# A fused attention, channel-mix and two-factor kernel: four-byte gate reads taken out of the load queue, and three numbers of the planner changed

## The chip, the core and the metric

One core of a Trainium2 chip runs the whole program. The metric is device time in microseconds, the median of several runs; lower is better. The engines are TensorE (PE, with its weight loads PEld beside it), VectorE (DVE), ScalarE (ACT), GpSimd (POOL) and SyncE (SP). SP computes nothing here: it issues every DMA of the kernel, one after the other, and each may first wait on semaphores.

## What is computed

Three blocks follow each other, on 4 batches of 576 positions:

```python
# 1: windowed attention, 8 heads of 64; heads 0-3 plain window of 32, heads 4-7 dilated by 4
scores = np.where(masks, scale * np.matmul(q, k.transpose(0, 1, 3, 2)), -1000000000.0)
attn = softmax(scores)                       # written out with max, exp, sum
x = np.matmul(attn, v)                       # -> x: (4, 576, 512)
# 2: channel mix with a shift by one position
xk = mu_k * x + (1.0 - mu_k) * x_prev
xr = mu_r * x + (1.0 - mu_r) * x_prev
k = np.maximum(xk @ w_k, 0.0)
x = sigmoid(xr @ w_r) * (k * k @ w_v)
# 3: a rank-32 product along the sequence, then two dense layers
u = x + (x.transpose(0, 2, 1) @ U @ V).transpose(0, 2, 1)
return u + np.maximum(u @ w_ch1, 0.0) @ w_ch2
```

The weights arrive as 64-bit numbers. The kernel turns them into fp32 itself, and splits most operands into a high and a low fp32r part, so that one product is three matmuls.

## The kernel before

The work of block 2 is cut into 8 chunks of 288 positions (two for each batch), that of block 3 into 5 groups of positions. Attention is cut into 32 units (a batch, one of two parts of the sequence, a pair of heads); units 0 to 3 run one by one in `attend`, the others in pairs in `attend2`. Chunk 0 of block 2 is multiplied in fp32 as it is (`L829` for the four r rows, `L813` for the k and v tiles); from chunk 1 on the split operands are used (`L816` to `L818`). So the first chunk needs only the 20 converted weight pieces (called W0 to W19 below; 512 KB of 64-bit words each), and the later ones need high and low parts of them (`L351`, `L348`).

One conversion is one ACT instruction (`L384`) and four on DVE (`L385`, `L386`, `L388`, `L391`). A k tile of chunk 0 needs four pieces, W4 to W7 for the first half of the tiles and W8 to W11 for the second; the v tiles need W12 to W15 and then W16 to W19.

The inputs come through `load`: q and k of a unit (`L522`, tile `raw`), v of a unit (`L525`, same tile), a weight piece (`L367`, tile `w`), the constants and mu. `raw` and `w` have four buffers each. A new unit's load must wait until PE has used up an old unit (`L603` or `L716`, the product with v); a new weight piece must wait until DVE has finished an old conversion (`L391`). From the 5th load to the 28th, `load` issues a gate first (`L336`): a DMA of four bytes, read out of the tile that the load four places earlier fills, which SP can issue only when that load has landed. So SP never runs more than four loads ahead there. Besides the gates, SP waits before a DMA when the DMA eight places earlier has not landed (semaphores `DMAHW0` to `DMAHW7` in the orders below).

Every instruction is recorded as an `op` with an expected duration, and `plan` sets the order. It simulates the five engines, picks on each engine among the next 160 operations the one that can start first or that is most urgent, and repeats that ten times with due times from the pass before. The order that it finds is the order in which the program is written; at run time each engine works its own list in that order, and waits where an operand is missing. In the planner a DMA takes size / `RATE`, one after the other, and a tile's buffer counts as free 40 ns after the last use of the tile that held it.

Near the end of block 2 and in group 0 of block 3 the converted `w_ch1` and `w_ch2`, parked in DRAM as `w2f`, come back (`L444`, tile `st`) and are combined for a seven-product scheme by DVE (`L471`), ACT (`L351`, `ch`) and POOL (`L346`, `cl`); `ug` (`L970`) holds a group of u, from which the operands `tr`, `tA` and `tB` are made.

Of the kernel before, what the change touches and what calls it, by code (L numbers as in the profile page):

```python
# [9 lines left out]
I32 = mybir.dt.int32  # L10
# [6 lines left out]
P = 128  # L17
# [8 lines left out]
QW, KW = 64, 96  # L26
# [6 lines left out]
NALL = NMASK + len(TWO)  # L33
# [18 lines left out]
QKW, VW = 640, 640  # L52
# [13 lines left out]
SLACK = 100.0  # L66
SLACK_PE = 100.0

OUTSTANDING = 4
GATED = 28  # L70
PLAN_PRINT = None
PASSES = 10
RATE = 245.0


@with_exitstack
def tile_attention_mix_channel(
    ctx: ExitStack, tc: tile.TileContext, qk0, qk1a, qk1b, v0, v1, cst, mu, w1raw, w2raw, upk, vpk, out
):
    nc = tc.nc  # L80
# [7 lines left out]
    cst_t = cp.tile([P, P + NALL * KW], F32, name="cst_t")  # L88
    ident = cst_t[:, 0:P]
    masks = [cst_t[:, P + i * KW : P + (i + 1) * KW] for i in range(NALL)]  # L90
    mu_t = cp.tile([P, 8], F32, name="mu_t")
# [7 lines left out]
    ops = []  # L99
# [21 lines left out]
    def op(eng, ns, fn, r=(), w=(), more=100, lock=False, mode=None, size=0):  # L121

        o = Op()
        o.eng, o.ns, o.fn, o.r, o.w, o.more, o.lock, o.mode, o.size = eng, ns, fn, list(r), list(w), more, lock, mode, size
        ops.append(o)

    def plan():
# [28 lines left out]
        def x_end(x):  # L156
            if x.end is not None:
                return x.end
            end = 0.0
            for u in reversed(x.ops):  # L160
                if u.done is None:
                    return NEVER
                end = max(end, u.done)
            x.end = end
            return end

        def ready(o):
            t = 0.0
            for d in o.deps:
                if d.done is None:  # L170
                    return None
                t = max(t, d.done + 40)
            if getattr(o, "behind", None) and o.behind.done is None:
                return None
            for x in o.tiles:
                if x.ops[0] is not o and x.ops[0].done is None:
                    return None
            for x in o.first:
                if x.at and x.line[x.at - 1].ops[0].done is None and x.line[x.at - 1].ops[0] is not o:
                    return None  # L180
                ends = sorted((x_end(y) for y in x.line[: x.at]), reverse=True)
                if len(ends) >= x.bufs:
                    if ends[x.bufs - 1] == NEVER:
                        return None
                    t = max(t, ends[x.bufs - 1] + 40)
            return t

        def forward(rank):
# [12 lines left out]
            while len(order) < len(ops):  # L201
# [32 lines left out]
                if e == "SP":  # L234
                    begin = max(t + 1300, dma)
                    dma = begin + o.size / RATE
                    o.done = dma + 700
# [85 lines left out]
    def dma(nbytes, fn, r, w):  # L323
        op("SP", 415, fn, r, w, size=nbytes)

    landing = []
    gate_d = tc.dram_tile([1, 64], I32, name="gate_d")

    def load(nbytes, fn, key, at):

        k = len(landing)
        landing.append((key, at))
        gate = None
        if OUTSTANDING <= k < GATED:
            seen, where = landing[k - OUTSTANDING]
            op("SP", 415, lambda: nc.sync.dma_start(gate_d[:, k : k + 1], where().bitcast(I32)[0:1, 0:1]),  # L336
               [seen], [("gate", k)], size=4)
            gate = ops[-1]
        dma(nbytes, fn, [], [key])
        ops[-1].behind = gate  # L340

    def sub(eng, n, out_, a, b, r, w, psum=False, fr=True):

# [20 lines left out]

    def cv_load(src, n):
        raw = Lazy([P, CW], I64, "w64", "w64", 4)
        load(P * n * 8, lambda: nc.sync.dma_start(raw()[:, :n], src), (raw,), lambda: raw())  # L367
        return raw

    def cv_bits(raw, n, xt_=None):  # L370
# [135 lines left out]
    def unit(u):  # L506
        part_i, pair = divmod(u, NPAIR)
        b, part = divmod(part_i, 2)
        return b, part, pair

    def a_load(u, which=("qk", "v")):
        b, part, pair = unit(u)
        nw, kc = unit_kind(pair, part)[:2]
        if part == 0:
            src, vsrc = qk0[b * NPAIR + pair], v0[b * NPAIR + pair]
        else:
            src, vsrc = (qk1a if pair < 2 else qk1b)[b * 2 + pair % 2], v1[b * NPAIR + pair]
        if u not in raws:
            raws[u] = Lazy([P, QKW + VW], F32, "raw", "raw", 4)
        raw = raws[u]  # L520
        if "qk" in which:
            load(P * 4 * (nw * QW + kc), lambda: nc.sync.dma_start(raw()[:, : nw * QW + kc], src),  # L522
                 (raw, "qk"), lambda: raw())
        if "v" in which:
            load(KW * 4 * 2 * nw * D, lambda: nc.sync.dma_start(raw()[:KW, QKW : QKW + 2 * nw * D], vsrc),  # L525
                 (raw, "v"), lambda: raw()[:, QKW:])

    def attend(u):
        b, part, pair = unit(u)
# [641 lines left out]
    def next_piece():  # L1171
        src, k, _ = jobs[len(loaded)]
        loaded.append(cv_load(src, k))

    a_load(0, ["qk"])
    load(P * 4 * (P + NALL * KW), lambda: nc.sync.dma_start(cst_t, cst), ("cst",), lambda: cst_t)
    next_piece()
    a_load(0, ["v"])
    load(P * 32, lambda: nc.sync.dma_start(mu_t, mu), ("mu",), lambda: mu_t)
    a_load(1, ["qk"])  # L1180
    next_piece()
    a_load(1, ["v"])
# [213 lines left out]
```

## Time and profile before

| | |
|---|---|
| device time, median of 3 runs | 775.2 us (773.4 to 776.62) |
| profiled execution: device time | 775.23 us |
| profiled execution: span | 773.3 us, so 1.93 us lie around it |
| PE busy | 740.0 us (96%) |
| PEld busy | 678.2 us (88%) |
| DVE busy | 580.5 us (75%) |
| ACT busy | 404.8 us (52%) |
| POOL busy | 396.1 us (51%) |
| mean granted clock of TensorE | 0.991 |

The shares are averages over stages with different limits: up to about 90 us attention, conversions and chunk 0 overlap; then the chunks 1 to 7 follow, and from about 360 us on block 3. A row of a timeline gives start and length of an instruction or of several equal ones, with the idle time ahead of it on its engine and what ended it in brackets.

### The profile page before, as it was taken

The numbers are of one execution on the slowest core, as the hardware profiler recorded it, in microseconds if no ns is written. First come the engines' busy times: TensorE is split into PE (matmuls) and PEld (weight loads), VectorE is DVE, ScalarE is ACT, GpSimd is POOL, SyncE is SP. The second block draws the span as 40 slices with busy tenths as digits, with TensorE's granted clock in tenths as the row PEclk, the third lists the DMA queues.
The fourth block names the chain that finished last, engine by engine and source line by source line (L and its number), as shares of the span: only waits on it lengthen the run. The fifth ranks groups of instructions, "written<-read, shape, count | busy, mean of one in ns | idle before, by whom it ended". The sixth has DMA issues, their size and how long they took to land. (4 is left out here: it accounts for less than half of the span.)

```text
span 773.3 us, 16141 instructions
## 1 busy us (share of the span) xinstructions
PE 740.0 (96%) x5784; PEld 678.2 (88%) x5784; DVE 580.5 (75%) x1302; ACT 404.8 (52%) x1019; POOL 396.1 (51%) x404
## 2 busy tenths in 40 slices
PE   4798999999999999999999999999999999999998
PEld 3566899999999999999898899889988999898986
DVE  5889989999999963556467889876797974665632
ACT  4578778767767765454345444443544343333310
POOL 1333236455646564355367668544677754455600
PEclk9989999999999999999999999999999999999999
DMA  8677627759685720345652344123442312032001
GB/s 251 207 230 227 202 71 236 231 169 288 207 271 177 235 90 31 106 129 178 202 196 79 103 155 141 54 89 97 144 135 69 122 56 82 29 110 82 28 1 54
DMA packets 54255, 107.56 MB, mean 139 GB/s; under 512 B 5920, under 2 KB 16032, under 8 KB 54176
## 3 DMA queue, kind: packets, MB, share of 16 engines
q1 hardware_dynamic: 54176, 106.54, 42.8%
q8 instruction: 45, 0.74, 0.4%
q14 instruction: 34, 0.28, 0.1%
HBM read 83.97 MB, written 22.54 MB: 138 GB/s over the span
## 5 line engine op out<-in xcount | busy, mean ns | idle before, releaser
L346 POOL TENSOR_TENSOR cl<-sums,ch 128x512 fp32r<-128x512 f32 x72 | 99.6, 1383 | 82.5 <-ACT ch L351 57.2
L1116 PE MATMUL psS<-hl,rh 128*128 128x512 f32 (+1 forms) x320 | 119.5, 373 | 2.0 <-DVE hl L1052 2.0
L1114 PE MATMUL psS<-hh,rh 128*128 128x512 f32 (+1 forms) x320 | 119.5, 374 | 1.7 <-ACT hh L1051 0.9
L1115 PE MATMUL psS<-hh,rl 128*128 128x512 f32 (+1 forms) x320 | 119.0, 372 | 0.0
L351 ACT ACTIVATE ch<-sums 128x512 fp32r<-128x512 f32 (+1 forms) x104 | 57.1, 561 | 113.3 <-DVE sums L471 104.7
L816 PE MATMUL psM<-xk,wh 128*128 128x288 f32 x336 | 101.2, 301 | 0.4 <-DVE y L878 0.4
L817 PE MATMUL psM<-xk,wl 128*128 128x288 f32 x336 | 99.1, 295 | 0.0
L818 PE MATMUL psM<-xk,wh 128*128 128x288 f32 x336 | 98.8, 294 | 0.0
L471 DVE TENSOR_TENSOR sums<-st 128x256 f32<-128x256 f32 (+1 forms) x144 | 90.5, 675 | 8.7 <-POOL cl L346 5.9
L346 POOL TENSOR_TENSOR cl<-st,ch 128x256 fp32r<-128x256 f32 x80 | 68.8, 876 | 54.6 <-PE psM L1039 31.4
L346 POOL TENSOR_TENSOR xk<-m,xk 128x288 fp32r<-128x288 f32 x56 | 52.4, 949 | 50.6 <-ACT xk L351 39.9
L1116 PEld LDWEIGHTS psS<-hl,rh 128*128 128x128 f32 x320 | 60.3, 188 | 14.0 <-DVE hl L1052 2.4
L1114 PEld LDWEIGHTS psS<-hh,rh 128*128 128x128 f32 x320 | 60.3, 188 | 12.2 <-DVE us L950 1.1
L346 POOL TENSOR_TENSOR k2s<-k,k2s 128x288 fp32r<-128x288 f32 x49 | 44.0, 900 | 48.8 <-ACT k2s L351 47.5
L1115 PEld LDWEIGHTS psS<-hh,rl 128*128 128x128 f32 x320 | 60.3, 189 | 9.5
L816 PE MATMUL psM<-k2s,wh 128*128 128x288 f32 x224 | 67.5, 301 | 0.0
L817 PE MATMUL psM<-k2s,wl 128*128 128x288 f32 x224 | 66.0, 295 | 0.0
L818 PE MATMUL psM<-k2s,wh 128*128 128x288 f32 x224 | 65.9, 294 | 0.0
L816 PEld LDWEIGHTS psM<-xk,wh 128*128 128x128 f32 x336 | 63.0, 188 | 1.4 <-DVE y L878 0.9
L818 PEld LDWEIGHTS psM<-xk,wh 128*128 128x128 f32 x336 | 63.2, 188 | 0.0
L817 PEld LDWEIGHTS psM<-xk,wl 128*128 128x128 f32 x336 | 63.1, 188 | 0.1
L1074 DVE TENSOR_TENSOR ok<-ok,psM 128x256 f32<-128x256 f32 (+1 forms) x96 | 46.4, 503 | 20.3 <-PE psM L1039 18.5
(156 smaller groups left out, 2146.8 us busy)
## 6 DMA issues: line engine op xcount, KB each, us to landing
st<-w2f SPq DMA_DIRECT2D x96, 256.0 KB, 3.1
w<-w2raw SPq DMA_DIRECT2D x32, 512.0 KB, 5.2
w<-w1raw SPq DMA_DIRECT2D x20, 512.0 KB, 5.2
w2f<-w SPq DMA_DIRECT2D x32, 256.0 KB
raw<-qk SPq DMA_DIRECT2D x16, 320.0 KB, 4.5
ytmp<-y SPq DMA_DIRECT2D x32, 144.0 KB, 2.1
yb<-ytmp SPq DMA_DIRECT2D x4, 1152.0 KB, 6.4
uf<-us SPq DMA_DIRECT2D x32, 144.0 KB, 2.4
```

The source lines that it names most:

```text
L346: op("POOL", t, lambda: nc.gpsimd.tensor_tensor(out=out_(), in0=a(), in1=b(), op=ALU.subtract), r, w, 40, lock=True)
L351: act(n, lambda: nc.scalar.activation(out_(), in_(), AF.Copy), r, w, psum, strided)
L471: dve(k * Q, lambda: nc.vector.tensor_tensor(out=q(sm_, n, k)(), in0=a(), in1=b(), op=op_), [(s1,), (s2,)], [(sm_, key)], two=True)
L816: nc.tensor.matmul(a, lhsT=wh, rhs=xh, start=start, stop=False)
L817: nc.tensor.matmul(a, lhsT=wl, rhs=xh, start=False, stop=False)
L818: nc.tensor.matmul(a, lhsT=wh, rhs=xl, start=False, stop=stop)
L1074: dve(k * Q, lambda: nc.vector.tensor_tensor(out=out_(), in0=a(), in1=b(), op=op_), r, w, two=True, psum=True)
L1114: nc.tensor.matmul(a, lhsT=wh, rhs=xh, start=(j == 0 and e == 0), stop=False)
L1115: nc.tensor.matmul(a, lhsT=wl, rhs=xh, start=False, stop=False)
L1116: nc.tensor.matmul(a, lhsT=wh, rhs=xl, start=False, stop=(j == 7 and e == 1))
```

## The change

The gates go, with the list of loads that they needed and the planner's rule that a load stands behind its gate. `RATE` goes from 245 to 285 GB/s. In `ready`, a tile first written by SP (a load of any kind into a reused buffer) is now taken to have its buffer 1,500 ns after the last use of the old tile instead of 40 ns; other engines keep 40. At run time nothing waits for these 1,500 ns: they only shape the order. Buffers, operations and sizes stay as they are, and every other line below `load` moves up by 15.

```diff
-OUTSTANDING = 4
-GATED = 28
+LATE = 1500.0
...
-RATE = 245.0
+RATE = 285.0
...
-            if getattr(o, "behind", None) and o.behind.done is None:
-                return None
...
-                    t = max(t, ends[x.bufs - 1] + 40)
+                    t = max(t, ends[x.bufs - 1] + (LATE if o.eng == "SP" else 40))
...
-    landing = []
-    gate_d = tc.dram_tile([1, 64], I32, name="gate_d")
-
-    def load(nbytes, fn, key, at):
-
-        k = len(landing)
-        landing.append((key, at))
-        gate = None
-        if OUTSTANDING <= k < GATED:
-            seen, where = landing[k - OUTSTANDING]
-            op("SP", 415, lambda: nc.sync.dma_start(gate_d[:, k : k + 1], where().bitcast(I32)[0:1, 0:1]),
-               [seen], [("gate", k)], size=4)
-            gate = ops[-1]
+    def load(nbytes, fn, key):
+
         dma(nbytes, fn, [], [key])
-        ops[-1].behind = gate
```

Since the order is planned anew, it moves on all engines. Three places follow; in the rows of the change a line number is 15 lower than that of the same line before.

On SP, from the load of W5 on (before). `w_333` is W5, `w_449` is W6; the two `qk1b` loads are units 6 and 7.

```order
L367 DMA w_333<-w1raw 128x512 [waits DVE_49,Activation_49]
L336 DMA gate_d<-w_285 1x1 [waits DMAHW5_49,DMAHW4_49]
L336 DMA gate_d<-raw 1x1 [waits DMAHW7_49]
L522 DMA raw<-qk1b 128x640 [waits DMAHW6_49,PE_49]
L525 DMA raw<-v 96x512
L336 DMA gate_d<-raw 1x1 [waits DMAHW1_49,DMAHW0_49]
L336 DMA gate_d<-w_333 1x1 [waits DMAHW3_49]
L522 DMA raw<-qk1b 128x640 [waits DMAHW2_49,PE_49]
L525 DMA raw<-v 96x512
L336 DMA gate_d<-raw 1x1 [waits DMAHW6_49,DMAHW4_49]
L367 DMA w_449<-w1raw 128x512 [waits DMAHW5_49,DVE_49,Activation_49]
```

The same stretch of the change: `w_307` is W5, `w_347` to `w_440` are W6 to W9, `qk1a` is unit 5.

```order
L352 DMA w_307<-w1raw 128x512 [waits DMAHW1_49,DVE_49,Activation_49]
L507 DMA raw<-qk1a 128x544 [waits DMAHW2_49,PE_49]
L510 DMA raw<-v 96x512 [waits DMAHW3_49]
L507 DMA raw<-qk1b 128x640 [waits DMAHW4_49,PE_49]
L510 DMA raw<-v 96x512 [waits DMAHW5_49]
L352 DMA w_347<-w1raw 128x512 [waits DMAHW6_49,DVE_49,Activation_49]
L352 DMA w_353<-w1raw 128x512 [waits DMAHW7_49,DVE_49,Activation_49]
L352 DMA w_425<-w1raw 128x512 [waits DMAHW0_49,DMAHW1_49,DVE_49,Activation_49]
L352 DMA w_440<-w1raw 128x512 [waits DVE_49]
L507 DMA raw<-qk1b 128x640 [waits DMAHW2_49,PE_49]
```

W5 now stands ahead of unit 5, and W6 to W9 stand ahead of unit 7 instead of behind it.

On PE, from the scores of units 6 and 7 to the first product of chunk 1 (before). `L654` are scores, `L699` transposes, `L716` products with v, `L813` with `xk` the k tiles and with `k` the v tiles.

```order
L654 MATMUL psS<-raw 64x96 x16
L813 MATMUL psM<-xk_248,wx 128x288 x16
L699 MATMUL psS<-cst_t,pr 96x128 x8
L716 MATMUL psS<-pts,raw 64x64 x16
L654 MATMUL psS<-raw 64x96 x20
L813 MATMUL psM<-xk_248,wx 128x288 x16
L813 MATMUL psM<-k_615,wx 128x288 x16
L699 MATMUL psS<-cst_t,pr 96x128 x10
L716 MATMUL psS<-pts,raw 64x64 x20
L654 MATMUL psS<-raw 64x96 x20
L813 MATMUL psM<-k_615,wx 128x288 x16
L816 MATMUL psM<-xk,wh 128x288
```

The same in the change:

```order
L639 MATMUL psS<-raw 64x96 x16
L798 MATMUL psM<-xk_239,wx 128x288 x16
L684 MATMUL psS<-cst_t,pr 96x128 x8
L798 MATMUL psM<-xk_239,wx 128x288 x4
L701 MATMUL psS<-pts,raw 64x64 x16
L639 MATMUL psS<-raw 64x96 x20
L798 MATMUL psM<-xk_239,wx 128x288 x12
L798 MATMUL psM<-k_610,wx 128x288 x8
L684 MATMUL psS<-cst_t,pr 96x128 x10
L798 MATMUL psM<-k_610,wx 128x288 x8
L701 MATMUL psS<-pts,raw 64x64 x20
L639 MATMUL psS<-raw 64x96 x20
```

Four matmuls of the k tiles now stand between transposes and the product with v, and eight of the v tiles behind the next transposes; the scores of units 6 and 7 keep their place among the tiles.

On SP in group 0 of block 3, from the `st` load of piece 10 of `w_ch1` (`w2f_80`) to `yb` of batch 2 (before):

```order
L444 DMA st<-w2f_80 128x512
L953 DMA uf<-us 128x288
L444 DMA st<-w2f_76 128x512
L444 DMA st<-w2f_81 128x512
L953 DMA uf<-us 128x288
L970 DMA ug<-uf 128x4x512
L953 DMA uf<-us 128x288
L444 DMA st<-w2f_79 128x512
L444 DMA st<-w2f_80 128x512
L953 DMA uf<-us 128x288 x2
L900 DMA yb<-ytmp_68 128x4x576
L444 DMA st<-w2f_82 128x512
```

The same in the change:

```order
L429 DMA st<-w2f_80 128x512
L429 DMA st<-w2f_81 128x512
L938 DMA uf<-us 128x288
L955 DMA ug<-uf 128x4x512
L429 DMA st<-w2f_76 128x512
L938 DMA uf<-us 128x288 x3
L429 DMA st<-w2f_79 128x512
L885 DMA yb<-ytmp_68 128x4x576
L429 DMA st<-w2f_80 128x512
L1113 DMA ot<-uf 128x256 x2
L429 DMA st<-w2f_82 128x512
```

`ug` has moved ahead of one `st` load; the second `st` load of piece 10 has moved behind `yb`, and two `ot` loads ahead of piece 12.

## Rows read from the trace of the kernel before

**Rows 1.** The page's DMA issues: operands, count, KB each, median us to landing.

```profile
st<-w2f SPq DMA_DIRECT2D x96, 256.0 KB, 3.1
...
yb<-ytmp SPq DMA_DIRECT2D x4, 1152.0 KB, 6.4
```

**Rows 2.** Busy time by stage: stretch, length, PE PEld DVE ACT POOL, clock, DMA share, GB/s.

```profile
0.00:43.44 43.44, 28.02 (x284) 20.93 (x284) 29.57 (x105) 23.14 (x83) 10.31 (x15) 0.88 0.74 233
43.44:90.36 46.92, 41.35 (x335) 32.08 (x331) 46.27 (x133) 37.02 (x100) 18.04 (x19) 0.96 0.73 224
90.36:355.00 264.64, 261.58 (x2526) 254.92 (x2525) 215.79 (x567) 178.78 (x502) 137.85 (x157) 1.00 0.54 172
355.00:440.00 85.00, 79.63 (x618) 76.02 (x618) 58.07 (x97) 38.46 (x79) 51.05 (x48) 1.00 0.47 150
440.00:769.70 329.70, 329.37 (x2031) 294.23 (x2030) 230.05 (x403) 127.43 (x258) 178.82 (x167) 1.00 0.25 85
```

**Rows 3.** What PE waited for from 43 to 91 us: total, times, longest.

```profile
PE psM L813 <- DVE wx L391: 3.6, 2, 2.9
PE psS L716 <- ACT pts L351: 1.2, 2, 0.7
```

**Rows 4.** Timeline of PE: start, length, line, operands, idle time before and its releaser.

```profile
14.39 1.04 PE L545 MATMUL psS<-raw 64*64 64x96 f32 x20 [2.15 <-DMA raw<-qk]
...
43.44 0.89 PE L654 MATMUL psS<-raw 64*64 64x96 f32 x32
...
46.65 6.57 PE L813 MATMUL psM<-xk,wx 128*128 128x288 f32 x26 [0.67 <-DVE wx L391]
...
57.56 1.88 PE L654 MATMUL psS<-raw 64*64 64x96 f32 x40
...
72.00 6.57 PE L813 MATMUL psM<-k,wx 128*128 128x288 f32 x26 [2.92 <-DVE wx L391]
...
81.72 1.06 PE L654 MATMUL psS<-raw 64*64 64x96 f32 x40
...
90.36 0.51 PE L816 MATMUL psM<-xk,wh 128*128 128x288 f32 x1
```

**Rows 5.** Timeline of SP's DMA issues from unit 6 to W9.

```profile
29.45 0.36 SPq L522 DMA_DIRECT2D raw<-qk1b  x1
...
32.55 0.36 SPq L522 DMA_DIRECT2D raw<-qk1b  x1
...
33.81 0.35 SPq L367 DMA_DIRECT2D w<-w1raw  x1
```

**Rows 6.** Timeline of ACT, DVE and POOL around two late conversions.

```profile
24.50 0.69 DVE L391 SCALAR_TENSOR_TENSOR wx<-w,wx 128x512 int32<-128x512 int32 x1
...
36.46 1.04 DVE L391 SCALAR_TENSOR_TENSOR wx<-w,wx 128x512 int32<-128x512 int32 x1
...
40.29 0.67 ACT L384 ACTIVATE wx<-w 128x512 f32<-128x512 f32 x1 [4.55 <-DMA w<-w1raw]
...
40.98 0.43 DVE L385 TENSOR_SCALAR wx<-wx 128x512 f32<-128x512 f32 x1 [2.06 <-ACT wx L384]
...
70.41 2.38 POOL L684 TENSOR_TENSOR pr<-pr,sm 128x480 f32<-128x480 f32 x2
...
70.62 1.33 DVE L391 SCALAR_TENSOR_TENSOR wx<-w,wx 128x512 int32<-128x512 int32 x1
```

**Rows 7.** The line of the gates (ns min/median/max) and landing times of `raw` loads.

```profile
L336 SPq DMA_DIRECT2D gate_d<-raw x16: 227/234/291, 3.6 to 36.6; - x16
...
DMA to landing us min/median/max: 2.9/4.4/8.0
```

**Rows 8.** Group 0 of block 3: the load of `ug`, POOL behind it, PE.

```profile
373.52 0.53 SPq L970 DMA_DIRECT2D ug<-uf  x1
...
381.98 1.80 POOL L346 TENSOR_TENSOR tA<-ug,tA 128x512 fp32r<-128x512 f32 x1 [12.68 <-ACT tA L351]
...
ACT rh L351 <- DMA st<-w2f: 2.6, 2, 1.9
```

More of the change, by code (lines that the diff above doesn't have):

```diff
@@ L366, in cv_load @@
         raw = Lazy([P, CW], I64, "w64", "w64", 4)
-        load(P * n * 8, lambda: nc.sync.dma_start(raw()[:, :n], src), (raw,), lambda: raw())
+        load(P * n * 8, lambda: nc.sync.dma_start(raw()[:, :n], src), (raw,))
         return raw
@@ L522, in a_load @@
             load(P * 4 * (nw * QW + kc), lambda: nc.sync.dma_start(raw()[:, : nw * QW + kc], src),
-                 (raw, "qk"), lambda: raw())
+                 (raw, "qk"))
         if "v" in which:
             load(KW * 4 * 2 * nw * D, lambda: nc.sync.dma_start(raw()[:KW, QKW : QKW + 2 * nw * D], vsrc),
-                 (raw, "v"), lambda: raw()[:, QKW:])
+                 (raw, "v"))
     def attend(u):
@@ L1175, in tile_attention_mix_channel @@
     a_load(0, ["qk"])
-    load(P * 4 * (P + NALL * KW), lambda: nc.sync.dma_start(cst_t, cst), ("cst",), lambda: cst_t)
+    load(P * 4 * (P + NALL * KW), lambda: nc.sync.dma_start(cst_t, cst), ("cst",))
     next_piece()
     a_load(0, ["v"])
-    load(P * 32, lambda: nc.sync.dma_start(mu_t, mu), ("mu",), lambda: mu_t)
+    load(P * 32, lambda: nc.sync.dma_start(mu_t, mu), ("mu",))
     a_load(1, ["qk"])
```

## The prediction

> **What bounds the kernel now.** I read the busy time by stage first, then the waits of PE, then the timelines at the waits that are left. PE is the bound: from 440 us to its last matmul at 769.7 us it is idle for 0.3 us of 329.7, and from 90.36 to 355 us for 3.1 of 264.6 [rows 2]. No order of loads can shorten what is full there. PE's idle time lies in two places. Up to 90.36 us, where chunk 1 begins, it is idle for 15.4 us (43.44 - 28.02) and then for 5.6 us (46.92 - 41.35); and from 355 to 440 us, in the first group of block 3, for 5.4 us (85.00 - 79.63) [rows 2]. In the second stretch of the opening DVE is busy for 46.27 of 46.92 us: there DVE, with the conversions, sets the pace, and PE waits for it.
>
> The waits say which conversions. From 43 to 91 us PE waited 3.6 us for `L391`, the last step of a conversion, in two pieces [rows 3]: 0.67 us before the k tiles at 46.65, which need W7, and 2.92 us before the v tiles at 72.00, which need W15 [rows 4]. The rest of the waits in that stretch (`L716` for ACT) is the latency of the attention chain.
>
> Why was DVE late? It stood idle for 2.06 us at 38.9, waiting for ACT, and ACT for the load of W6: 4.55 us, until 40.29 [rows 6]. W6's buffer had been free since W2's conversion ended at 24.50 + 0.69 = 25.2 [rows 6], but SP issued the load only at 33.81, since the loads of units 6 and 7 stood ahead of it and waited for PE; they went at 29.45 and 32.55 [rows 5]. So W6 came 8.6 us later than its buffer would have allowed, because of SP's order.
>
> **The change part by part.** The gates themselves: 24 DMAs of some 0.23 us each on SP [rows 7], 5.5 us in all, and waits for landings between them. SP computes nothing, and until 38 us it mostly waits for buffers anyway, so what counts is only which load comes earlier. In the opening the first loads are all queued early in both versions and land in the same order. Without gates the third unit's q and k could come sooner; PE waited 2.15 us for them at 14.39 [rows 4]. That bounds this part at 0 to -2.2 us. I take 0: the PE order keeps the scores of units 6 and 7 as one fixed point (43.44, [rows 4]), and these need the load of unit 7, which now stands behind W6 to W9; what is won before is waited away there.
>
> That load is the part that can cost. Before, it went out at 32.55 [rows 5]. Now W9 stands ahead of it, and needs the buffers of W4 and W5, whose conversions ended by 36.46 + 1.04 = 37.5 [rows 6]. In the new DVE order the same point comes with two `L770` and one small pair less ahead of it, and with less idle time, so I put it at 36 us. With the longest landing of a `raw` load, 8.0 us [rows 7], unit 7 is there at 44.0, with the median of 4.4 us at 40.4; PE wants it at 43.44. So the cost is 0 to +0.6 us; if the point stays at 37.5, up to 45.5 - 43.44 = +2.1. W8 and W9 lie in the same queue, so I lean to the long end, near which the scores come just in time: 0.
>
> W6 itself now follows unit 6 directly: issued at about 30.3 instead of 33.81, 3.5 us sooner. ACT had waited until 40.29, so it is ready by 36.8 at the same landing time, before DVE gets there at 38.9. The 2.06 us of idle time [rows 6] go, and DVE fills them with conversions.
>
> What the k and v tiles then see: the new DVE order runs W6 to W9 before the scores of units 6 and 7, where before only W6 and part of W7 were done. So W7 is ready long before the k tiles (0.67 us gone), and W15, with two pieces less left after 47 us and a conversion costing 0.43 + 0.43 + 0.69 + 0.69 = 2.2 us where POOL does not hold it up (the two shorter steps by the 0.43 us of the `L385` in [rows 6], the longer by 0.69), comes some 4.5 us sooner against the 2.92 us that PE waited. Both waits go: **-3.6 us**. The scores of those units come later on DVE by as much, but their normalised rows were wanted by PE only after 8 us of k tiles, and the new order lets the pair's transposes be followed by four matmuls of k tiles, which cover the wait of `L716`. What is late next is this attention chain: ACT's 1.2 us of [rows 3], which I leave as they are.
>
> The clock: the scores at 57.56 took 1.88 us, the same 40 records at 81.72 1.06 us [rows 4]; the granted clock of that stretch is 0.96 on average [rows 2], that is, part of it at 1.2 GHz instead of 2.4. With PE busy without a break this 0.8 us could go. Bounds 0 to -0.8; I take 0, since PE's waits for attention stay.
>
> After 90.36 the order of all engines is planned anew, but what they do is the same. In group 0 of block 3 POOL stood idle for 12.68 us until 381.98, waiting for `ug` (issued at 373.52), and is then the engine that PE waits for [rows 8]. In the new order one `st` load of 256 KB less stands ahead of `ug`. At the 233 GB/s of the first stretch [rows 2] that is 1.1 us, at the 285 of the planner 0.9. Part of it reaches PE: between 0 and -1.1, I take **-0.5**. Nothing else there is worth a figure of its own; re-ordered waits of PE in the stage, 5.4 us in all, are the bound for their change to the better, and the third rival is the one to the worse.
>
> Sum: 773.3 - 3.6 - 0.5 = 769.2 us of span, and with the 1.93 us around it **771.1 us**. The profiled execution (775.23) lies on the median (775.2), so nothing is added. That is -0.53%; a difference of over 0.5% is about what a measurement of this kernel can tell from none, and 0.5% is 3.9 us, so the forecast lies just beyond that edge.
>
> **The rivals.** *Given back.* PE reaches chunk 1 sooner, but its split operands are also DVE's and POOL's work, and DVE was full (46.27 of 46.92, [rows 2]). DVE itself wins only the 2.06 us of W6 and what it can put off; if the 3.6 us turn up again as waits of `L816` for `L348` or `L346`, 775.2 - 0.5 = 774.7 us remain. For it: how full DVE is. Against it: in the new DVE order fewer of the `L348` stand before the first products of chunk 1, so that work has been put off, not only moved. The conversion of W15 took 1.33 us for its last step instead of 0.69 while POOL normalised from 70.41 on [rows 6]; such collisions may meet another conversion in the new order, and two of them (0.64 us each) would by themselves bring back 1.3 us. The Trainium skill, "SBUF — State Buffer", section "Who interferes with whom", says why: a DVE instruction with two SBUF inputs and a GpSimd instruction that reads SBUF exclude each other for a whole instruction. By that rule the time is not saved by moving, only paid elsewhere, and this rival is the result; the row agrees that the step doubled.
>
> *Unit 7 late.* If its load lands 3.0 us after 43.44 (issued at 38.4, [rows 6] with W5's end and SP's turn, and 8.0 us to land), PE stands there with nothing else in its order: 771.1 + 3.0 = 774.1 us. The Trainium skill, "DMA: Bandwidth & Descriptors", section "Latency and other measured facts", gives an access latency of 0.2 us on average and 2 us at high load. By it a fuller queue would add up to 1.8 us to each landing, an estimate from that page; the rows have no fuller queue to compare.
>
> *Slower: loads of block 3 too late.* The planner now believes that an `st` buffer is free 1.5 us late, and puts such loads behind others: the second load of piece 10 behind `yb`, piece 12 behind two `ot`. `yb` is 1152 KB and takes 6.4 us to land, an `st` load 3.1 us [rows 1]. Where PE works just behind POOL, each load that comes late by its landing costs PE 3.1 us; three such places without cover make 771.1 + 9.3 = 780.4 us. It decides where DVE, ACT or POOL come to `st` before it lands. Before, ACT waited for `st` twice, 2.6 us in all [rows 8], so there is a cushion, but not a large one; and the first of the three uses is not urgent by the order.
>
> *More.* If the 2.15 us of the opening and the 0.8 us of the clock are kept as well: 771.1 - 3.0 = 768.1 us.
>
> **How the numbers follow.** Forecast, 771.1 us with its own spread of 768.9 to 773.3: 0.46. More, 768.1: 0.15. Given back, 774.7, with the case that the order does nothing at all: 0.20. Unit 7 late, 774.1: 0.05. Slower, 780.4: 0.14. Faster by over 0.5% (below 771.3): 0.15 and 0.29 of the forecast's 0.46, so 0.44. Within: 0.17 + 0.20 + 0.05 = 0.42. Slower: 0.14. The range of 766.5 to 779.0 takes in the more favourable case with 1.6 us of spread and the lighter half of the slow one, and leaves out about 0.15.
>
> **What would show it.** In the profile of the changed kernel: no wait of `L813`'s successor line (`L798`) for a conversion above 0.7 us; no ACT wait of 4 us for the load of a weight piece near 40 us; scores of units 6 and 7 on PE no later than 44.5 us; the first product of chunk 1 at 86 to 88 us instead of 90.36; PE's idle time from chunk 1 to the end close to the 8.8 us of before (3.1 + 5.4 + 0.3). The forecast is wrong if chunk 1 begins at 90 us or later (the conversions did not come sooner, or unit 7 did not come), if it begins sooner and PE then waits for `wl` or `xk` (given back), or if PE is idle for 9 us or more in the first group of block 3 (late loads).

## The result, and the profile after

The changed kernel takes 765.0 us (763.81 to 767.06, six runs) against 774.97 us (773.4 to 776.78) of the kernel before beside it: a ratio of 0.9871, with a 95% interval of 0.985 to 0.9891. The forecast was 771.1 us with a range of 766.5 to 779.0. The direction was right; the gain is 10 us instead of 4, and the time lies 1.5 us below the range. The profiled execution took 765.21 us, its span 763.4.

The busy time by stage, divided as in [rows 2]: at the scores of units 6 and 7, at the first product of chunk 1, 11.2 us ahead of the first product of block 3, 85 us behind that, and at PE's last product (stretch, length, PE, PEld, DVE, ACT, POOL, clock, DMA share, GB/s):

```profile
0.00:45.63 45.63, 28.52 (x284) 20.95 (x284) 32.28 (x114) 24.85 (x85) 9.69 (x15) 0.89 0.77 238
45.63:88.61 42.98, 40.72 (x345) 31.41 (x341) 41.58 (x128) 36.76 (x112) 16.62 (x20) 1.00 0.76 237
88.61:349.12 260.51, 258.53 (x2507) 252.38 (x2505) 210.63 (x565) 177.06 (x489) 140.99 (x158) 1.00 0.55 174
349.12:434.12 85.00, 84.32 (x662) 81.33 (x662) 61.05 (x99) 38.73 (x79) 52.84 (x50) 1.00 0.48 156
434.12:759.41 325.29, 324.73 (x1999) 289.65 (x1997) 223.17 (x398) 125.71 (x255) 173.69 (x163) 1.00 0.25 84
```

Against [rows 2]: units 6 and 7 come 2.2 us later (45.63 for 43.44); the stretch from there to chunk 1 is 3.9 us shorter, and PE is idle in it for 2.3 us instead of 5.6; in the first group of block 3 PE is idle for 0.7 us instead of 5.4. Up to chunk 1 DVE was busy for 73.9 us instead of 75.8, with 242 instructions for 238.

The timeline of PE that answers [rows 4] (start, length, operands, idle time ahead and its releaser):

```profile
42.41 2.21 PE L814 MATMUL psM<-xk,wx 128*128 128x288 f32 x8 [2.48 <-DVE xk L755]
45.63 0.89 PE L639 MATMUL psS<-raw 64*64 64x96 f32 x32
46.45 8.03 PE L798 MATMUL psM<-xk,wx 128*128 128x288 f32 x32
...
59.13 1.05 PE L639 MATMUL psS<-raw 64*64 64x96 f32 x40
...
66.04 4.04 PE L798 MATMUL psM<-k,wx 128*128 128x288 f32 x16
...
77.29 8.48 PE L798 MATMUL psM<-k,wx 128*128 128x288 f32 x32
85.80 0.75 PE L684 MATMUL psS<-cst_t,pr 128*96 128x128 f32 x5
88.10 0.75 PE L684 MATMUL psS<-cst_t,pr 128*96 128x128 f32 x5 [1.55 <-POOL pr L669]
88.61 0.38 PE L801 MATMUL psM<-xk,wh 128*128 128x288 f32 x1
```

No `L798` waits for a conversion; from 43 to 91 us PE waits for POOL only (`pr`, 1.55 and 0.61 us). The scores at 59.13 take 1.05 us where the same 40 took 1.88 [rows 4], in a stretch with a granted clock of 1.00 where it was 0.96. The last v tile ends at 85.8 us instead of 90.7 (82.71 + 8.03); then ten transposes follow that stood behind the first products of chunk 1 before.

SP's issues that answer [rows 5] (W6 to W9 in one row, then unit 7), and the longest wait of DVE for a conversion's first step from 20 to 90 us, of before and of after:

```profile
27.03 9.70 SPq L352 DMA_DIRECT2D w<-w1raw  x4
38.97 0.33 SPq L507 DMA_DIRECT2D raw<-qk1b  x1
```

```profile
DVE wx L385 <- ACT wx L384: 2.1, 1, 2.1
```

```profile
DVE wx L370 <- ACT wx L369: 0.3, 1, 0.3
```

And block 3, answering [rows 8]: `ug` on SP, POOL's first work on it, and ACT's wait for `st`:

```profile
363.73 0.53 SPq L955 DMA_DIRECT2D ug<-uf  x1
...
371.19 1.82 POOL L331 TENSOR_TENSOR tA<-ug,tA 128x512 fp32r<-128x512 f32 x1 [9.82 <-ACT tA L336]
...
ACT rh L336 <- DMA st<-w2f: 1.9, 3, 0.8
```

The first product of block 3 begins at 360.3 us (366.2 before), so in relation to PE `ug` goes out 3.9 us earlier. The waits of PE around that group (330 to 440 us), before and after:

```profile
PE psS L1116 <- DVE hl L1052: 2.0, 2, 1.7
PE psS L928 <- POOL yl L917: 0.9, 1, 0.9
PE psS L1114 <- ACT hh L1051: 0.9, 1, 0.9
PE psS L1114 <- DVE us L950: 0.6, 1, 0.6
PE psM L1038 <- POOL cl L346: 0.5, 1, 0.5
PE psM L928 <- POOL yl L917: 0.4, 1, 0.4
```

```profile
PE psM L1022 <- DVE ok L1059: 0.3, 1, 0.3
PE psS L1101 <- DVE hl L1037: 0.2, 1, 0.2
```

So PE's idle time fell in three places, the opening, the first group of block 3 and, less, the stretch between them, and I had priced only the first two. The experiments have to say which part of the change does it in each.

### The profile page after: what moved, and what is told of

It reads as the page before. It is cut to its first block, busy times and chain, and to the rows that moved or that the text cites. A ratio compares the mean times of both kernels' runs of the same rounds, so it can differ in the third digit from the quotient of the medians.

```text
span 763.4 us, 16086 instructions
## 1 busy us (share of the span) xinstructions
PE 736.8 (97%) x5784; PEld 675.7 (89%) x5784; DVE 569.5 (75%) x1302; ACT 403.1 (53%) x1017; POOL 393.8 (52%) x404
## 5 line engine op out<-in xcount | busy, mean ns | idle before, releaser
L331 POOL TENSOR_TENSOR cl<-sums,ch 128x512 fp32r<-128x512 f32 x72 | 97.7, 1357 | 80.9 <-ACT ch L336 53.1
L331 POOL TENSOR_TENSOR cl<-st,ch 128x256 fp32r<-128x256 f32 x80 | 66.4, 845 | 57.5 <-PE psM L1024 37.8
L456 DVE TENSOR_TENSOR sums<-st 128x256 f32<-128x256 f32 (+1 forms) x144 | 87.2, 654 | 10.5 <-POOL cl L331 5.8
```

The source lines that it names most:

```text
L331: op("POOL", t, lambda: nc.gpsimd.tensor_tensor(out=out_(), in0=a(), in1=b(), op=ALU.subtract), r, w, 40, lock=True)
L456: dve(k * Q, lambda: nc.vector.tensor_tensor(out=q(sm_, n, k)(), in0=a(), in1=b(), op=op_), [(s1,), (s2,)], [(sm_, key)], two=True)
```

## The experiments

All are made from the kernel before, whose `plan` got its numbers as arguments, `plan(ops, RATE, LATE, gated, given)`; line numbers are 5 higher than before in the first eight, 13 higher in the others. "Old order" is `plan(ops, 245.0, 40.0, True)`, "new order" `plan(no_gates, 285.0, 1500.0, False)`; they give each engine the lists of the two kernels. The code shows the lines that matter, with ... where lines are left out; `no_gates` is the list of operations without the gates. The table has the median, the kernel before on the same chip, the ratio with its interval, and from the profiled execution three stretches: to the first split product of chunk 1, from there to the first product of block 3, and from there to the end, each with PE's idle time. The last idle time has in it the 3.5 to 4.1 us behind PE's last product.

| run | us | before | ratio | to chunk 1 (idle) | to block 3 (idle) | to the end (idle) |
|---|---|---|---|---|---|---|
| before | 775.2 | | | 90.4 (21.0) | 275.8 (3.9) | 407.1 (8.4) |
| after | 765.0 | 774.97 | 0.9871 [0.985, 0.9891] | 88.6 (19.4) | 271.7 (2.0) | 403.1 (5.2) |
| e1 | 775.63 | 774.73 | 1.001 [0.9989, 1.003] | 91.7 (20.2) | 274.3 (2.7) | 405.4 (6.9) |
| e2 | 774.89 | 774.73 | 0.9992 [0.9975, 1.001] | 90.7 (23.6) | 277.7 (4.6) | 403.5 (5.6) |
| e3 | 772.99 | 774.73 | 0.9984 [0.9959, 1.0009] | 90.1 (17.1) | 275.2 (5.0) | 404.4 (6.7) |
| e4 | 771.04 | 774.73 | 0.9959 [0.994, 0.9978] | 95.0 (21.2) | 272.3 (2.5) | 403.1 (5.3) |
| e5 | 763.91 | 776.1 | 0.9848 [0.9813, 0.9883] | 88.9 (21.8) | 269.1 (0.1) | 404.8 (6.4) |
| e6 | 774.38 | 776.1 | 0.9988 [0.997, 1.0005] | 93.4 (20.8) | 273.8 (2.4) | 404.7 (6.0) |
| e7 | 774.08 | 776.1 | 0.997 [0.9954, 0.9986] | 89.3 (20.2) | 278.1 (5.3) | 405.0 (6.6) |
| e8 | 780.02 | 776.1 | 1.0057 [1.0035, 1.0079] | 92.4 (22.8) | 274.3 (2.7) | 410.1 (10.7) |
| e9 | 768.78 | 774.88 | 0.9919 [0.9894, 0.9945] | 91.6 (21.9) | 271.9 (1.1) | 402.4 (4.7) |
| e10 | 770.75 | 774.88 | 0.9945 [0.9918, 0.9972] | 89.2 (19.2) | 274.7 (4.4) | 404.0 (6.1) |
| e11 | 772.44 | 774.88 | 0.9959 [0.9928, 0.9989] | 93.5 (23.2) | 270.6 (1.4) | 403.6 (5.2) |
| e12 | 770.61 | 774.88 | 0.9934 [0.9903, 0.9964] | 95.1 (23.5) | 269.5 (0.5) | 404.3 (6.0) |
| e13 | 763.93 | 775.98 | 0.9852 [0.9807, 0.9897] | 89.1 (18.9) | 269.8 (0.8) | 403.3 (5.3) |
| e14 | 765.32 | 775.98 | 0.9866 [0.9826, 0.9907] | 88.6 (19.4) | 269.1 (0.2) | 404.4 (5.9) |
| e15 | 766.48 | 775.98 | 0.9881 [0.9844, 0.9918] | 86.0 (18.8) | 275.8 (3.8) | 402.3 (4.7) |
| e16 | 766.59 | 775.98 | 0.9881 [0.9844, 0.9917] | 87.3 (20.1) | 273.7 (2.0) | 403.4 (5.8) |
| e17 | 760.92 | 773.98 | 0.9828 [0.9803, 0.9853] | 85.4 (17.5) | 272.0 (1.2) | 403.6 (5.5) |
| e18 | 764.26 | 773.98 | 0.9878 [0.9853, 0.9902] | 88.1 (17.8) | 269.5 (0.4) | 404.4 (5.9) |

In the new opening ten transposes stand ahead of chunk 1 that stand behind it in the old (two rows of 0.75 us above); so some 1.3 us of the difference between two kernels can be a move from the second stretch to the first. In e4 and e11 they stand ahead too, in e6, e7 and e15 to e17 behind. One order differs by 1 to 3 us from one profile to the next: the new one (after, e5, e18) has 88.1 to 88.9, 269.1 to 271.7 and 403.1 to 404.8, the old one (before, e1) 90.4 to 91.7, 274.3 to 275.8 and 405.4 to 407.1. So totals are judged by the medians.

**The reads alone** (e1: old order; e13: new order).

```diff
-        for o in plan():
-            o.fn()
+        for o in plan(ops, 245.0, 40.0, True):
+            if not getattr(o, "is_gate", False):
+                o.fn()
```

> The kernel before, planned as before, but the 24 gate reads are not issued; every engine keeps its order. Theory (the time went where the order changed; the reads themselves cost nothing, since SP waits for buffers in the opening anyway): 774.0 to 775.5 us, chunk 1 still begins near 90 us, PE still idle for about 5 us in the first group of block 3. Rival (the reads and the waits for landings behind them hold the loads up): 770 to 772 us, with the load of W6 issued earlier than 33.8 us and chunk 1 before 88 us.

Taking the 24 reads out of the old order gave a ratio of 1.001. In e13 they were put back into the new order, each ahead of its load:

```diff
+        loads_x = []
+        for o in plan(no_gates, 285.0, 1500.0, False):
+            if getattr(o, "where", None):
+                k = len(loads_x)
+                if OUTSTANDING <= k < GATED:
+                    nc.sync.dma_start(gate_d[:, k : k + 1], loads_x[k - OUTSTANDING]().bitcast(I32)[0:1, 0:1])
+                loads_x.append(o.where)
+            o.fn()
```

> The order of the changed kernel, with a four-byte read put back ahead of each load from the 5th to the 28th in SP's new order, out of the tile of the load four places earlier; nothing else moves. Theory (the reads cost nothing in either order, since SP waits for buffers there): 763.5 to 766 us. Rival (without the brake the first loads share the DMA engines, and unit 1's q and k came later, PE waited 4.8 to 6.1 us for them instead of 3.7): 761 to 763 us with the brake. Second rival (the brake costs, now that the weight pieces stand close together): 767 to 770 us.

763.93 us with the reads, 763.91 and 764.26 without (e5, e18). At run time they cost nothing that these runs can tell, in either order. That is the theory; the rivals of both runs fall.

**Two halves spliced** (e2, e3). One order up to 200 us of the planner's time, then what is left of the other.

```diff
...
+        cut_x = next(i for i, (o, t) in enumerate(order_x) if t >= CUT)
+        front_x = [o for o, t in order_x[:cut_x]]
+        seen_x = set(map(id, front_x))
+        for o in front_x + [o for o, t in order_y if id(o) not in seen_x and not getattr(o, "is_gate", False)]:
+            o.fn()
```

> Both orders are planned; up to 200 us of the planner's time the old order (with its gates) is issued, behind that all that is left in the new order. Theory (two separate gains of about 4.7 us each, one up to chunk 1 and one in the first group of block 3, the second from the order of block 3 alone): 770 to 771 us, PE idle 15.4 and 5.6 us in the two stretches of the opening as before and under 1.5 us in the first group of block 3. Rival (block 3 goes better only because everything arrives there earlier from the opening): 774.5 to 775.5 us, with PE idle for 4 to 6 us in that group.

> The other way round: the new order (no gates) up to 200 us of the planner's time, then what is left in the old order. Theory (two separate gains): 769.5 to 771 us, chunk 1 begins at 85 to 87 us, PE idle for 4 to 6 us in the first group of block 3. Rival (the gain of block 3 comes out of the opening): 765 to 766 us.

Neither came as the theory had it: both are within 0.3% of before. By stretch, block 3 follows its order (PE's waits from 330 to 440 us are 1.0 us in e2 and 3.9 in e3), but from chunk 1 to 330 us PE waits 3.3 us for `k` of block 2 in e3 and 2.2 us for `pr` in e2, waits of which neither kernel has more than 0.2 us there. A splice is no clean cut of a plan, and as totals the two say nothing.

**One number at a time** (e4, e6, e7, e11). Three numbers are named in the title, but `plan` has two that change, `RATE` and the time for a load's buffer; the third part is the rule that a load stands behind its gate. One line of each run, with its label:

```diff
+        for o in plan(ops, 285.0, 1500.0, True):           # e4
+        for o in plan(no_gates, 245.0, 1500.0, False):     # e6
+        for o in plan(no_gates, 245.0, 40.0, False):       # e7
+        for o in plan(no_gates, 285.0, 40.0, False):       # e11
```

> The kernel before with RATE 285 and 1500 ns for a load's buffer, gates kept and planned with. Theory (the two numbers make the order; the gates only keep SP from running more than four loads ahead, which the buffers do as well): 764 to 768 us. Rival (the gates bind the opening: with them the loads of W6 to W9 cannot move ahead): 769.5 to 771 us, the gain of block 3 alone.

> No gates, RATE stays 245, only the 1500 ns for a load's buffer are new. The order of SP around ug (the load of group 1 of block 3) is then that of the changed kernel, while in the opening units 6 and 7 still stand ahead of the loads of W8 and W9. Theory (the 1500 ns put ug ahead of the loads that wait for their buffers, and that makes the gain in block 3; the opening is a matter of the order there): PE idle under 1.5 us in the first group of block 3 and 768 to 771 us in all. Rival (the gain in block 3 needs RATE 285 too): 773 to 775 us.

> The order planned without gates and with the old numbers, 245 and 40. In block 3 the two st loads stand ahead of ug as before; in the opening W3 to W5 come earlier, W6 to W9 hardly. Theory: 772.5 to 775.5 us, with PE idle for 3.5 to 5.5 us in the first group of block 3. Rival (the freedom from the gates in the plan is what changes the opening): 769 to 771 us, chunk 1 before 88 us.

> No gates, RATE 285, a load's buffer free after 40 ns as before. The order has two loads of weight pieces ahead of unit 7 instead of four, and one st load between the uf stores and ug. Theory (both numbers together bring W6 to W9 ahead of unit 7, one alone does not; and without the 1500 ns ug stays behind st loads): 770 to 774 us, with PE waiting 2 us or more for conversions. Rival (RATE is the number that matters): 764 to 767 us.

None of the four reaches the changed kernel; their gains are 2 to 4 us, and that of e6 is within its interval of none. e4 came out at its rival's time: the two numbers with gates in the plan give everything behind chunk 1 (272.3 and 403.1 us), but an opening that ends at 95.0 us. So the gates cost as a rule of the plan, not as DMAs. e6 falsifies the theory, its total (774.38) and the idle time (2.0 us in that group, not under 1.5): it has the new order of SP around `ug` and an opening that ends at 93.4 us. e7 is in its theory's range, with 2.3 us of idle time in that group, less than expected. With RATE 285 the second stretch takes 270.6 and 272.3 us (1.3 us more with the transposes counted in), with 245 273.8 and 278.1. In e11 PE waits 5.9 us for `pr` in the opening, not for conversions as expected; the total is in its range.

**Planned on from a state** (e9, e10). The opening of one order is given, and the rest planned from its state with the other's numbers, so nothing is left over at a seam. The lines are those of e9, where `rest_x` has no gates behind the opening; in e10 the numbers are the other way round.

```diff
+        opening = plan(ops, 245.0, 40.0, True)
+        opening = opening[: next(i for i, o in enumerate(opening) if o.mode == "f32r")]
...
+        for o in plan(rest_x, 285.0, 1500.0, True, opening):
+            o.fn()
```

> The old order with its gates is kept up to the first split product of chunk 1; from that state on the rest is planned with RATE 285 and 1500 ns. Unlike in the splice no work is left over at a seam. In block 3 SP's order around ug is that of the changed kernel. Theory (two gains: some 3 us up to chunk 1, the rest behind it from the order there): 768 to 771 us; chunk 1 at 90 to 92 us, PE idle under 1.5 us in the first group of block 3. Rival (all depends on the opening): 774 to 776.5 us.

> The new order up to the first split product of chunk 1, and from that state on planned with the old numbers, 245 and 40 (there are no gates behind the opening in either). In block 3 the two st loads stand ahead of ug again. Theory (two gains): 769.5 to 773 us; chunk 1 at 88 to 90 us, PE idle for 3 to 5 us in the first group of block 3. Rival (all depends on the opening): 764 to 767 us.

768.78 and 770.75 us beside 774.88: with the old opening the new rest brings 6.1 us (interval 4.3 to 8.2), with the new opening a rest by the old numbers 4.1 (2.2 to 6.4), and the two add up to the 10 us of the whole. The theory holds, the rival (all hangs on the opening) falls. In e9 the second stretch is 2.4 us shorter than in the same opening with the old rest (e1, 274.3), the third 3.0. e10 is the less clean of the two: its rest is a new plan by the old numbers, not the old lists. Its third stretch is 1.4 to 3.1 us shorter than in the old order, and PE is idle for 1.7 us in the first group of block 3 where 3 to 5 were expected, so part of its 4.1 us may be won there.

**Single loads moved on SP** (e8, e12, e14). In finished orders, with the lists of the other engines kept. The code is that of e8 and e12; e14 puts one `st` load ahead of the last `uf` store and of `ug` in the same way.

```diff
+        order = plan(ops, 245.0, 40.0, True)                             # e8
...
+        late_x = [o for o in sp[at_ug - 3 : at_ug] if o.size == P * CW * 4]
+        for o in late_x:
+            order.remove(o)
+        i_ug = order.index(sp[at_ug])
+        order[i_ug + 1 : i_ug + 1] = late_x
...
+        order = plan(no_gates, 285.0, 1500.0, False)                     # e12
...
+        late_x = loads_x[8:10]
+        for o in late_x:
+            order.remove(o)
+        i_v7 = order.index(v7)
+        order[i_v7 + 1 : i_v7 + 1] = late_x
```

> The order of the kernel before, gates included, with one edit: the two st loads that stand right ahead of the last uf store and of ug in group 0 of block 3 are put behind ug. No other engine changes its order. In the kernel before SP stood 2.78 us at these two. Theory (SP's wait there holds up ug, and with it ACT, DVE and POOL, on which PE waits later): ug is issued some 3 us earlier in relation to PE, the 4 to 5 us of idle PE in that group shrink to 1 to 3, 771 to 773 us. Rival (PE's waits there are those of its own order, products right behind their conversions; ug is only one of many loads): 774 to 776 us, PE's waits for hh, hl and cl as before.

e8 became slower, 780.02 us, which neither theory nor rival had. The issues of SP, the wait of DVE and those of PE (330 to 440 us):

```profile
369.58 2.10 SPq L958 DMA_DIRECT2D uf<-us  x2
374.64 0.52 SPq L975 DMA_DIRECT2D ug<-uf  x1
375.21 1.08 SPq L449 DMA_DIRECT2D st<-w2f  x2
```

```profile
381.68 1.29 DVE L353 TENSOR_TENSOR rl<-st,rh 128x512 fp32r<-128x512 f32 x2 [5.95 <-ACT rh L356]
```

```profile
PE psS L1119 <- DVE us L955: 6.2, 2, 5.8
...
PE psS L1121 <- DVE hl L1057: 0.2, 1, 0.2
```

`ug` was not issued sooner: 7.9 us behind the first product of block 3 (366.7), 7.3 before. It waits for the last `uf` store, and that for DVE's `us` row, not for the `st` loads. The two loads came late, and in DVE's list `rl`, which needs them, stands ahead of the `us` rows, for which PE waited 5.8 us. The waits for `hl` and `hh` of the old order shrank to 0.2 us, with PE stopped ahead of them.

> The order of the changed kernel with one edit on SP: the st load that stands behind ug in group 0 of block 3 is put ahead of the last uf store and of ug again. No other engine changes its order. Theory (SP waits there for the st buffer, 1.4 us in the changed kernel, and ug and all that hangs on it come later by that): ug issued 1.5 to 3 us later in relation to PE, PE idle for 1 to 3 us more in that group, 765 to 767.5 us. Rival (in the new order ACT, DVE and POOL have that much room): 763.5 to 765 us.

Putting the `st` load ahead of `ug` again in the new order costs at most 1.4 us: 765.32 against 763.91 to 764.26, with intervals that overlap. The total is in the theory's range, but its reason is not there: `ug` goes out 3.5 us behind the first product of block 3 as in the changed kernel (3.4). So its place among the `st` loads does not set when `ug` goes out. Neither edit moved that time by more than 0.6 us, so whether PE gains by an earlier `ug` was not tested. The rows of before point to one place where it would. ACT waited for `ug`, and `hh` stood behind that in its list, though the products for it had ended at 380.9; then PE waited for `hh` (ACT, then PE):

```profile
381.27 1.15 ACT L351 ACTIVATE tA<-ug 128x512 fp32r<-128x512 f32 x2 [5.42 <-DMA ug<-uf]
...
384.97 1.07 ACT L1051 ACTIVATE hh<-psM 128x512 fp32r<-128x512 f32 x2
```

```profile
385.60 0.38 PE L1114 MATMUL psS<-hh,rh 128*128 128x256 f32 x1 [0.86 <-ACT hh L1051]
```

Over all profiles the two go together: with `ug` 6.7 to 7.9 us behind the first product of block 3, PE is idle in that group for 3.6 to 7.7 us (before, e1, e3, e8), with 5.4 to 5.8 us for 1.7 to 2.3 (e7, e10, e11), with 2.8 to 4.3 us for 0.3 to 2.0 (all others). That is no proof, since whole plans differ.

> The order of the changed kernel with one edit on SP: the loads of W8 and W9 are put behind the two loads of unit 7, the other engines keep their order. Theory (the weight pieces ahead of unit 7 are what lets PE run without waiting for conversions): unit 7 comes some us earlier, W8 and W9 later; PE waits 1.5 to 4 us for conversions again before chunk 1, 766 to 768 us. Rival (the order on PE and DVE makes the opening, the loads have room): 763 to 765.5 us.

With W8 and W9 behind unit 7 the new order takes 770.61 us; the price is larger than theory and rival had it. ACT got its piece late, DVE stood for it, and the fourth r row waited for `xk` of DVE (DVE, ACT, PE):

```profile
46.17 0.43 DVE L398 TENSOR_SCALAR wx<-wx 128x512 f32<-128x512 f32 x1 [6.47 <-ACT wx L397]
```

```profile
45.48 0.66 ACT L397 ACTIVATE wx<-w 128x512 f32<-128x512 f32 x1 [5.09 <-DMA w<-w1raw]
```

```profile
47.08 4.21 PE L842 MATMUL psM<-xk,wx 128*128 128x288 f32 x8 [7.43 <-DVE xk L783]
```

Late weight pieces stop the opening, as the theory says, but through DVE's list and an r row that needs neither of the two pieces, not through PE's tiles. Chunk 1 begins at 95.1 us.

**Other plans near it** (e15, e16, e17; e5 and e18 are the new order beside them).

```diff
+        for o in plan(no_gates, 330.0, 2000.0, False):     # e15
+        for o in plan(no_gates, 285.0, 500.0, False):      # e16
...
+        opening = plan(no_gates, 330.0, 2000.0, False)     # e17
+        opening = opening[: next(i for i, o in enumerate(opening) if o.mode == "f32r")]
+        for o in plan(no_gates, 285.0, 1500.0, False, opening):
```

> No gates, RATE 330 and 2,000 ns. The planner then reckons with chunk 1 starting 5 us earlier than by the numbers of the changed kernel. Theory (the loads did 230 to 260 GB/s in the opening, so a plan for 330 asks for weight pieces before they can be there; behind the opening PE is full anyway): 764 to 769 us, chunk 1 no earlier than 88 us, from there on as in the changed kernel. Rival (a plan that wants loads earlier is also better where they come late): 758 to 763 us.

> No gates, RATE 285, and 500 ns instead of 1,500 for a load's buffer. Theory (RATE 285 alone already gives the stretch behind the opening, what differs is the opening, by a few us either way): from chunk 1 to the end 673 to 676 us as in the changed kernel, 763 to 771 us in all. Rival (the 1,500 ns are what block 3 needs): 677 us or more from chunk 1 to the end.

> The order of the changed kernel once more, beside the three others of this call, since the kernel before has shown 771 to 779 us from run to run. Both theories: 764 to 766.5 us; chunk 1 begins at 88 to 90 us, PE idle under 1 us in the first group of block 3.

766.48 and 766.59 us. Both stand in their theory's range of totals, but not by its reasons. In e15 chunk 1 came at 86.0 us, not at 88 or later, and the time from there to the end is 678.1 us instead of the 674.8 of the changed kernel. In e16 that time is 677.1 us, by the letter the rival's side (677 or more) and not the theory's 673 to 676. But 1.3 us of either are the transposes, which the changed kernel has ahead of chunk 1, and what is longer in e16 is the second stretch, not block 3, which the rival had named: e16 decides neither way. No fixed rule on RATE follows from it. e5 came at 763.91 us with chunk 1 at 88.9, but PE idle for 1.9 us in the first group of block 3, not under 1: that much the same order differs by.

> The opening planned with 330 and 2,000 up to the first split product of chunk 1, and from that state on planned with 285 and 1,500. The plan for 330 brought chunk 1 to 86.0 us but took longer behind it. Theory (opening and rest can be chosen apart, as the two runs that were planned on showed): chunk 1 at 86 to 88 us, 761 to 764 us in all. Rival (what the opening for 330 wins it leaves undone for the chunks behind it): 764.5 to 767 us.

> The order of the changed kernel beside it, for a comparison on the same chip: 763.5 to 766 us by both.

760.92 us, all six runs (758.87 to 762.75) below all six of the new order beside it (763.82 to 766.71). The opening for 330 keeps its lead when the rest is planned with 285 and 1,500. It is the fastest kernel here. In its opening the load of unit 7 stands between W8 and W9; before it stood ahead of W6, in the changed kernel behind W9:

```profile
31.98 0.33 SPq L535 DMA_DIRECT2D raw<-qk1b  x1
32.35 1.14 SPq L538 DMA_DIRECT2D raw<-v  x1
33.59 11.10 SPq L380 DMA_DIRECT2D w<-w1raw  x5
```

## Why the prediction was right, and where it was wrong

*The gates, 0:* right, in both orders. PE's wait for the third unit's q and k (2.15 us) is gone, but its wait for the second unit's grew from 3.65 to 4.76. What I didn't see is that the gates bound the plan (e4).

*W6 and the conversions, -3.6:* right in its rows, and about right in size, the size in part by luck. DVE's 2.06 us are 0.3, and PE's waits for `L391`, 3.6 us, are gone. But units 6 and 7 began at 45.63, not by 44.5, since the r rows now wait 5.4 us for `xk` where they waited 2.5; and chunk 1 began at 88.6, not by 88, since ten transposes and a wait of 1.55 us for `pr` stand ahead of it. So chunk 1 came only 1.75 us sooner in the two profiles, some 3 us if the transposes are counted out. What made up for the new waits is PE's own work: its busy time to chunk 1 is 69.2 us with the ten transposes, 69.4 without them before, some 1.4 us less for the same matmuls, at a mean granted clock of 0.94 instead of 0.92. I had left the clock at 0. e10, whose opening is this one, brought 4.1 us in all.

*Unit 7, 0:* right, but not by my sum. Its load went out at 38.97, not at 36, and landed 4.3 us later, at 43.2, not after the 8.0 us that I had leaned to; and PE came to its scores at 45.63. That the errors made up for each other is luck.

*Given back:* it did not happen. The work put off behind chunk 1 did not come back as waits: idle time from there to block 3 fell from 3.9 to 2.0 us. The Trainium skill, "SBUF — State Buffer", section "Who interferes with whom", had made this rival likelier. The exclusion is in the rows: a `rl` pair of DVE took 2.30 us at 381.22, beside a step of POOL, and 1.28 us at 401.68 with POOL idle in the changed kernel. What it cost in the opening no run separates.

*Slower by late `st` loads:* it did not happen here; ACT waited 1.9 us for `st`, 2.6 before. That two `st` loads in a wrong place can do it, e8 shows: ACT's wait for `st` there was 7.7 us.

*Block 3 and everything behind chunk 1, -0.5:* **the step that failed.** I wrote that all engines are planned anew "but what they do is the same", and priced one edge, `ug` by one `st` load, at 1.1 us at most. The new rest alone brought 6.1 us (e9, interval 4.3 to 8.2). The sum had named 5.4 us of idle time in the first group as "the bound for their change to the better" and then taken nothing of it, and it took nothing of the 3.1 us from chunk 1 to 355 us. In the profiles idle time behind chunk 1 fell from 12.3 to 7.2 us, 5.1 in all; these two have in them the 3.6 and 4.0 us behind PE's last product, which my 8.8 us left out.

The edge was mis-sized and its path misread. `ug` came 3.9 us sooner in relation to PE, not 1.1, and not because of the `st` load (e8, e14): it waits for the last `uf` store. And POOL is not "the engine that PE waits for": of PE's 5.3 us of waits, 1.8 are for POOL, 2.6 for DVE and 0.9 for ACT. What is shown is that the old order leaves PE idle in the first group for 3.9 to 5.4 us (e1, before; 3.6 in e3), and every other plan tried for 0.3 to 2.3 us. Among these are e7 and e10, whose block 3 is planned by the old numbers: for 1.7 and 2.3 us it takes no new number, only another plan. Which edge removes each wait stays open. The waits for `hl`, 1.5 to 2.0 us, stand in the five profiles where both numbers are old behind chunk 1 (before, e1, e3, e7, e10), and are 0.3 us at most in the others (also in e8, with the old order but PE stopped ahead of them). The second stretch stays open too: with the transposes counted in, it is 1 to 4 us shorter than in the old order with RATE 285 in e4, e9 and e11, 1 to 2 us with 500 ns (e16), and not with 330 (e15).

*The range:* it ended 1.5 us above the result because no case had a gain behind chunk 1 beyond 0.5 us. Taking half of the 8.5 us of idle time that I had named would have moved the forecast to 767.4. The exact time could not be had this way: plans with numbers near these took 760.9 to 774.4 us, so how good the one plan is that the new numbers draw is partly chance.

## What to carry to other kernels

A number that a planner uses rewrites the order of every engine to the end of the program. So price such a change by all the idle time of the bounding engine, stretch by stretch, and not by the two or three places where the difference of the orders catches the eye. To test one part, keep an opening and plan on from its state: moving two loads in a finished order cost 4 to 6 us (e8, e12), and the two splices came out at the time of before. And openings and rests can be chosen apart: e17, put together from two plans, beat both kernels.

## What was not expected of the hardware

Without the reads the first loads take longer to land, and that costs nothing, since they also go out sooner. The second to fourth loads of q and k (320 KB each) took 3.6, 6.1 and 4.9 us from issue to landing in the new order with the reads put back (e13), and 7.6, 9.3 and 8.7 us without them (e18). But they were issued at 5.4, 9.3 and 14.3 us in e13 and at 3.1, 5.3 and 9.8 in e18. So they landed at 9.0, 15.4 and 19.2 us with the reads and at 10.7, 14.5 and 18.5 without, and the totals are 763.93 and 764.26 us. In the first 30.8 us of e13 the DMA engines were busy for 0.78 of the time at 239 GB/s, in the first 31.0 of e18 for 0.85 at 248. The landing of these three loads, in e13 and then in e18:

```profile
DMA to landing us min/median/max: 3.6/4.9/6.1
```

```profile
DMA to landing us min/median/max: 7.6/8.7/9.3
```

The Trainium skill, "DMA: Bandwidth & Descriptors", section "Latency and other measured facts", gives an access latency of up to 2 us at high load, from which I had estimated up to 1.8 us more for a landing. By these rows a landing grew by 3.1 to 4.0 us; it has in it the time behind other loads, which that figure leaves out.
